# Four neighbouring rows per partition: loads in longer pieces, stores to every fourth row, and a last transpose on TensorE

## The chip, the cores and the metric

The kernel runs on one core of a Trainium2 chip. The metric is the device time of one execution in microseconds (us); the time before is the median of three runs. One further execution was taken by the hardware profiler; its span runs from the first to the last instruction.

## The reference

Attention that keeps the 32 largest scores of each query row, then a feed-forward layer with a squared ReLU. All inputs and the output are float32.

```python
# q, k, v: (8 batches, 8 heads, 576 rows, 64);  w_in: (512, 2048);  w_out: (2048, 512)
scores = scale * np.matmul(q, k.transpose(0, 1, 3, 2))
kth = np.partition(scores, -32, axis=-1)[..., -32:-31]
scores = np.where(scores >= kth, scores, -1e9)
attn = softmax(scores)
x = (attn @ v).transpose(0, 2, 1, 3).reshape(8 * 576, 512)
h = np.maximum(x @ w_in, 0.0)
return (h * h) @ w_out          # (4608, 512)
```

The order of the keys of one head doesn't change a row's result, as long as k and v have the same order. The order of the query rows changes only the row of the output that a result belongs to.

## The kernel before

**A plan, written out.** The kernel first builds a list of operations (`Plan.op`, L73 on), each with an engine, an estimated duration, a priority, the tiles that it reads and writes and the buffers that it takes. `Plan.schedule` (L141) is a list scheduler: it walks through time by events, gives each free engine the ready operation with the lowest priority number, and so fixes the order of the instructions on each of the five queues (PE, ACT, DVE, GpSimd named POOL, and SP for the DMAs). `Emitter` numbers the semaphores and writes the instructions in that order. At run time each engine works through its own list and waits only on semaphores. The scheduler's durations are constants in the code; a load counts the same whatever its pieces are.

**Loads.** A head pair is two heads of one batch. `load_pair` (L653) loads q, k and v of a pair. Four blocks of 128 rows and a rest of 64 rows make up the 576 rows. In the tile of q or k a partition holds five blocks times two heads times 64 elements (`rq`, `rk`: `[P, 5, 2, D]`); in that of v it holds four blocks of the first head, four of the second, and the rests (`rv`: `[P, 10, D]`). A 512-row load gives partition p the rows p, 128 + p, 256 + p and 384 + p:

```python
nc.sync.dma_start(r[:, 0:4, h, :], src[b, 2 * hp + h, r0:r0 + 512, :].rearrange("(tb p) d -> p tb d", p=P))
```

The first pair has its own loads, spread over two queues (`load_first`, L597), with the first block of q by itself (`both`). Its transposes come after ten warm-up matmuls on ones (L1384) in TensorE's order. TensorE transposes each 128-row block (L585), ACT copies the result to `qk`.

**Groups.** A group is 128 query rows of both heads of a pair, or the 64 rest rows of two pairs; there are 144. `score` (L719) makes 576 scores per row and head, ACT copies them to `s` (L755). `top_k` (L835) finds the 32nd largest: DVE folds four quarters of 144 columns into their maxima (L905), POOL gets the smaller ones by integer adds and subtracts (L900), and DVE draws eight maxima at a time (L939, L934, L946) and replaces them (L943). ACT makes the mask `w` from the threshold (L965; L952 and L955 for the last group), TensorE transposes the scores (L585) and adds the mask (L582), ACT takes the exponential `p` (L1021), and `fetch` multiplies by v. Four groups (`HUNT`) get their threshold by a search on ACT and POOL in place of the folds.

**The test and the second plan.** The folds may miss a value, for instance when more than eight of the 32 largest lie in one part. `verdict` (L1388) tests all rows at the end and leaves one flag. If it is set, all engines branch into a second plan (`again`, L1465), which finds all 144 groups' thresholds by full-width maxima and writes all of the output again.

**From attention to the feed-forward layer.** `gather` (L1078) collects the products in `av`. `collect` (L1090) divides by the sums on POOL (L1096) and transposes `x` into `xt` by a DMA (L1109). `feed` (L1121) and, for the last chunk, `feed_last` (L1184) run the two matrix products over chunks of up to 256 rows; `feed_last` accumulates over the head pairs as they come, so that its early matmuls (L1190) need the first two pairs only. In the last chunk the third pair is transposed by TensorE already (L1100), and the fourth in `collect_last` (L1062). Stores go out per 128 rows from two `o` buffers (L1180), for the last chunk in two halves of 256 columns (L1245).

Of the kernel before, what the change touches and what calls it, by code (L numbers as in the profile page):

```python
# [13 lines left out]
P = 128  # L14
# [370 lines left out]
def bass_top_k_attn__then__act_relu_squared_kernel(  # L385
# [8 lines left out]
    NB, H, S, D = q.shape  # L394
# [6 lines left out]
    NHP = 4  # L401
# [187 lines left out]
    def build(full, weights, pl):  # L589
# [7 lines left out]
        def load_first(b, hp, rq, rq2, rk, base):  # L597

            def part(t, src, h, tb, n_):
                r0 = 128 * tb + (64 if h and src is k else 0)  # L600
                return at(t)[:, tb:tb + n_, h, :], src[b, 2 * hp + h, r0:r0 + 128 * n_, :].rearrange(
                    "(tb p) d -> p tb d", p=P)

            def rest(t, src, r0, d0):
                x = src[b, 2 * hp, r0:r0 + 64, :]
                return at(t)[0:64, 4, :, :], bass.AP(x.tensor, x.offset, [x.ap[0], [(S + d0) * D, 2], x.ap[1]])

            def start(queue, *parts):
                return lambda: [queue.dma_start(*x()) for x in parts]

            both = bass.AP(q.tensor, q[b, 2 * hp, 0:P, :].offset, [[D, P], [S * D, 2], [1, D]])
            pl.op("sp", .1, base - 82, start(nc.scalar, lambda: part(rk, k, 0, 0, 4),
                                             lambda: rest(rk, k, REST[0], REST[1] - REST[0])),
                  w=[rk], take=[rk], sem=slot_sem, ndma=2, via="act")
            pl.op("sp", 4.0, base - 81, start(nc.sync, lambda: part(rk, k, 1, 0, 4)), w=[rk], sem=lambda o: "first", ndma=1)
            pl.op("sp", 3.5, base - 80, start(nc.sync, lambda: (at(rq)[:, 0, :, :], both)), w=[rq], take=[rq],
                  sem=slot_sem, ndma=1)
            pl.op("sp", 3.5, base - 79, start(
                nc.sync, lambda: part(rq2, q, 0, 1, 3), lambda: part(rq2, q, 1, 1, 3), lambda: rest(rq2, q, 512, 0)),
                w=[rq2], take=[rq2], sem=slot_sem, ndma=3)  # L620
# [32 lines left out]
        def load_pair(b, hp, base):  # L653
# [3 lines left out]
            def load(t, src, rest):  # L657
                def fn():
                    r = at(t)
                    res = []  # L660
                    for h in range(2):
                        r0 = 64 if h and rest != (512, 512) else 0
                        res.append(nc.sync.dma_start(r[:, 0:4, h, :], src[b, 2 * hp + h, r0:r0 + 512, :].rearrange(
                            "(tb p) d -> p tb d", p=P)))
                    x = src[b, 2 * hp, rest[0]:rest[0] + 64, :]
                    res.append(nc.sync.dma_start(r[0:64, 4, :, :], bass.AP(
                        x.tensor, x.offset, [x.ap[0], [(S + rest[1] - rest[0]) * D, 2], x.ap[1]])))
                    return res
                return fn

            def loadv():
                r = at(rv)
                res = [nc.sync.dma_start(r[:, 4 * h:4 * h + 4, :], v[b, 2 * hp + h, 64 * h:64 * h + 512, :].rearrange(
                    "(tb p) d -> p tb d", p=P)) for h in range(2)]

                for h in range(2):
                    res.append(nc.sync.dma_start(r[64 * h:64 * h + 64, 8 + h, :], v[b, 2 * hp + h, REST[h]:REST[h] + 64, :]))
                return res
# [411 lines left out]
        def collect(got, tt, quick):  # L1090

            avs, nu, xr = got["avs"], got["n"], tile("x")
            r0, rzs_ = units(nu)
            rz = pl.op("dve", .07 + .0045 * nu, tt + 4, lambda: vec.reciprocal(rzall[:, r0:r0 + nu], at(avs)[:, 0:nu, 64]), r=[avs], late=LATE if not quick else 0)
            rzs.append(rz)
            pl.op("gp", .14 + .108 * nu, tt + 4, lambda: gp.tensor_tensor(  # L1096
                at(xr)[:, 0:nu, :], at(avs)[:, 0:nu, 0:64], rzs_, ALU.mult), r=[avs], w=[xr], take=[xr], after=[rz])
            (gi, u0, n_, (xt, col, first), hp) = got["parts"][0]
            if quick == 2 and hp == NHP - 2:
                x = Tile(psum)  # L1100
                pl.op("pe", .1, tt - 30, lambda: tr(half(x)[:, 0:64 * nu], flat(xr, 0, nu), ident_bf[:, :]), r=[xr], w=[x], take=[x])
                return [pl.op("act", .35, tt - 30, lambda: act.copy(
                    at(xt)[:, hp, col:col + 64 * nu], half(x)[:, 0:64 * nu]), r=[x], w=[xt])]
            ops = []
            rows = [p for p in got["parts"] if p[0] != Z]
            if rows:
                _, u0, n_, (xt, col, first), hp = rows[0]
                assert [p[1:3] + (p[4],) for p in rows] == [(u0, n_, hp), (u0 + n_, n_, hp + 1)]
                ops += 2 * [pl.op("sp", 2.0, tt + 5, lambda u0=u0, n_=n_, xt=xt, col=col, hp=hp: [nc.sync.dma_start_transpose(  # L1109
                    at(xt)[:, hp:hp + 2, col:col + 64 * n_].rearrange("p a (i q) -> p (a i) q", q=P) if n_ == 4 else  # L1110
                    at(xt)[:, hp:hp + 2, col:col + 64 * n_], flat(xr, u0, 2 * n_))], r=[xr], w=[xt],
                    take=[xt] if first else [], ndma=1, bw=.25 * n_, sem=lambda o: f"x{xr.slot}")]
# [6 lines left out]
            return ops  # L1119

        def feed(chunk, xt, tm, step):  # L1121

# [34 lines left out]
            for tb in range((nt + 127) // 128):  # L1157
# [17 lines left out]
                for b_, r0, m_ in chunk:  # L1175
                    lo_, hi_ = max(at_, 128 * tb), min(at_ + m_, 128 * tb + n_)
                    if lo_ < hi_:
                        rows.append((lo_ - 128 * tb, hi_ - lo_, S * b_ + r0 + lo_ - at_))
                    at_ += m_
                pl.op("sp", 2.3, to + lag + 4 * step + 1, lambda ob=ob, rows=rows: [nc.sync.dma_start(  # L1180
                    out[row:row + m_, :], at(ob)[p0:p0 + m_, :]) for p0, m_, row in rows],
                    r=[ob], ndma=len(rows), sem=lambda o: f"o{o.tiles[0].slot}")

        def feed_last(chunk, xt, tt, turns):  # L1184
# [56 lines left out]
            for e in range(2):  # L1241
# [1 line left out]
                pl.op("act", .42, tt, lambda e=e, half_=half_: act.copy(  # L1243
                    at(ob)[0:nt, half_], bank(ops[e])[0:nt, 0:256]), r=[ops[e]], w=[ob])
                pl.op("sp", 2.3, tt + e, lambda half_=half_: [nc.sync.dma_start(  # L1245
                    out[S * b + q0:S * b + q0 + nt, half_], at(ob)[0:nt, half_])], r=[ob], ndma=1, sem=lambda o, e=e: f"oe{e}")

        xts = [None] * len(CHUNKS)
        turned = {}
# [276 lines left out]
```

## Time and profile before

| | |
|---|---|
| median of three runs | 775.21 us (775.09 to 775.52) |
| profiled execution | 774.41 us |
| its span | 772.6 us |
| busy: DVE, ACT, PE, POOL | 751.6, 717.9, 713.3, 687.6 us |
| DMA moved | 52.63 MB, 145,033 packets, of which 137,088 under 512 B |

Read it so: four engines are busy for nine tenths of the span or so, and DVE for 97% of it. An edit that shortens a transfer matters where an engine that sets the end waits for it; so the places to look at are the waits for DMAs, and the two ends of the span, where DVE isn't busy yet or any more.

### The profile page before, as it was taken

How to read it: one execution, taken by the hardware profiler on the slowest of the kernel's cores; microseconds unless marked ns; L12 is line 12 of the kernel's file. 1: busy time of each engine (PE TensorE's matmuls, PEld its weight loads, DVE VectorE, ACT ScalarE, POOL GpSimd, SP SyncE). 2: the span in 40 equal slices, each digit the busy share in tenths (PEclk: the TensorE clock that was granted, in tenths of full speed). 3: DMA queues.
4: the chain of work that ended last, by engine and by line, in shares of the span. 5: the costliest groups of instructions: out<-in, count | busy, mean ns of one | idle time of the engine just before them, and what ended most of it. 6: DMA issues, size and time to landing. Idle time of an engine off the chain costs nothing.

```text
span 772.6 us, 27813 instructions
## 1 busy us (share of the span) xinstructions
PE 713.3 (92%) x10680; PEld 528.2 (68%) x10680; DVE 751.6 (97%) x3589; ACT 717.9 (93%) x1141; POOL 687.6 (89%) x720
## 2 busy tenths in 40 slices
PE   7888888999989999998999889999899999999999
PEld 3656666666666676666767657686677777767776
DVE  5999999999999999999999999899999999999996
ACT  4799989899899999999999999999999999998884
POOL 4898998889789899989999899899999998989991
PEclk9999999999999999999999999999999999999999
DMA  7657452032400134103340043301332021100101
GB/s 191 182 137 196 132 135 52 23 83 48 114 11 9 51 83 95 32 16 85 70 99 10 18 111 86 69 6 46 93 82 67 11 68 38 34 23 23 36 23 34
DMA packets 145033, 52.63 MB, mean 68 GB/s; under 512 B 137088, under 2 KB 137344, under 8 KB 144896
## 3 DMA queue, kind: packets, MB, share of 16 engines
q1 hardware_dynamic: 144224, 50.66, 26.7%
q8 instruction: 84, 1.38, 0.8%
q14 instruction: 53, 0.43, 0.2%
q10 hardware_dynamic: 672, 0.16, 0.1%
HBM read 36.70 MB, written 9.44 MB: 60 GB/s over the span
## 4 chain that ended last, share of the span: by engine, by line
ACT 58%; PE 31%; DVE 8%; issue 2%; DVEq 0%; ACTq 0%
PE ps L582 26%; ACT w L965 13%; ACT p L1021 12%; ACT s L755 12%; ACT g L1140 7%; PE ps L585 5%; ACT hz L776 4%; ACT g L1155 3%; DVE f L943 2%; DVE f L905 2%; ACT o L1172 2%; DVE c L939 2%; ACT av L1087 2%; ACT qk L711 1%; ACT qk L712 1%
## 5 line engine op out<-in xcount | busy, mean ns | idle before, releaser
L900 POOL TENSOR_TENSOR f<-u,f 128x864 int32<-128x864 int32 x138 | 236.7, 1715 | 7.6
L965 ACT ACTIVATE w<-s,kth 128x576 bf16<-128x576 f32 x278 | 220.2, 829 | 3.5 <-DVE kth L946 3.5
L943 DVE MATCH_REPLACE8 f<-c,f 128x98 f32<-128x98 f32 (+2 forms) x840 | 221.2, 270 | 0.0
L939 DVE MAX8 c<-f 128x8 f32<-128x98 f32 (+2 forms) x840 | 201.5, 272 | 0.0
L582 PE MATMUL ps<-qk 64*128 64x384 f32 (+3 forms) x1280 | 179.5, 427 | 6.9 <-DVE f L905 5.8
L900 POOL TENSOR_TENSOR u<-f,s 128x576 int32<-128x576 int32 x138 | 166.5, 1206 | 16.6 <-DVE f L905 15.9
L1021 ACT ACTIVATE p<-ps 128x1152 bf16<-128x1152 f32 x144 | 169.1, 1174 | 12.5 <-PE ps L582 11.9
L755 ACT COPY s<-ps 128x1152 f32<-128x1152 f32 x140 | 162.0, 1157 | 17.3 <-PE ps L582 16.9
L582 PEld LDWEIGHTS ps<-qk 64*128 64x128 f32 (+1 forms) x1280 | 130.5, 175 | 39.6 <-DVE f L905 11.8
L582 PE MATMUL ps<-wo,g 128*128 128x512 bf16 (+1 forms) x592 | 142.9, 375 | 2.7 <-ACT qk L714 1.2
L582 PE MATMUL ps<-xt,win 128*128 128x256 bf16 (+1 forms) x1280 | 132.5, 252 | 8.5 <-ACT g L1140 3.6
L900 POOL TENSOR_TENSOR u<-s 128x288 int32<-128x288 int32 x138 | 110.2, 799 | 29.8 <-ACT s L755 26.5
L905 DVE TENSOR_TENSOR f<-ps,f 128x288 f32<-128x288 f32 x280 | 123.7, 442 | 0.1
L946 DVE MAX8 kth<-f 128x8 f32<-128x296 f32 x280 | 120.7, 456 | 0.0
L585 PEld LDWEIGHTS ps<-ident,s 64*128 64x128 f32 x2520 | 96.8, 139 | 30.9 <-ACT w L965 15.1
L582 PEld LDWEIGHTS ps<-xt,win 128*128 128x128 bf16 x1280 | 97.2, 98 | 29.3 <-ACT g L1140 6.0
L934 DVE MAX8 f<-f 128x8 f32<-128x288 f32 x280 | 114.7, 447 | 0.0
L585 PE MATMUL ps<-ident,s 64*128 64x64 f32 x2520 | 107.0, 227 | 4.6 <-ACT w L965 4.1
L1152 POOL TENSOR_TENSOR g<-g 128x512 bf16<-128x512 bf16 x86 | 89.4, 1042 | 2.9 <-ACT g L1140 2.6
L582 PEld LDWEIGHTS ps<-wo,g 128*128 128x128 bf16 x592 | 49.6, 98 | 55.2 <-issue 5.7
L1140 ACT ACTIVATE g<-ps 128x512 bf16<-128x512 f32 x140 | 86.2, 641 | 1.0 <-PE ps L582 0.9
L582 PEld LDWEIGHTS ps<-vb,p 128*128 128x128 bf16 (+1 forms) x1600 | 54.0, 100 | 32.7 <-ACT g L1140 10.5
(104 smaller groups left out, 859.1 us busy)
## 6 DMA issues: line engine op xcount, KB each, us to landing
rv<-in_v_dram SPq DMA_DIRECT2D x64, 128.0 KB, 2.4
rk<-in_k_dram SPq DMA_DIRECT2D x63, 128.0 KB, 2.5
rq<-in_q_dram SPq DMA_DIRECT2D x62, 128.0 KB, 2.5
out_dram<-o SPq DMA_DIRECT2D x31, 256.0 KB, 2.2
g<-in_moe_w_in_dram SPq DMA_DIRECT2D x8, 512.0 KB, 4.2
g<-in_moe_w_out_dram SPq DMA_DIRECT2D x8, 512.0 KB, 4.3
out_dram<-o SPq DMA_DIRECT2D x10, 128.0 KB, 2.3
rq<-in_q_dram SPq DMA_DIRECT2D x32, 32.0 KB, 2.5
```

The lines of the kernel that those rows point to most:

```text
L582: return pe.matmul(o, l, r, start=start, stop=stop, skip_group_check=True)
L585: return pe.matmul(o, i, ident, is_transpose=True, skip_group_check=True, **kw)
L755: cp = [pl.op("act", 1.1, tg - LEAD + 1, lambda: act.copy(at(st)[:, :, 0:S], two(banks(ss)[:, FIRST_AT:], SECOND, S)), r=[ss], w=[st])]
L900: return pl.op("gp", dur, prio, lambda: gp.tensor_tensor(o().bitcast(I32), x().bitcast(I32), y().bitcast(I32), op), **kw)
L905: return dve(.36, lambda: vec.tensor_tensor(o(), two(banks(ss)[:, FIRST_AT + c:], SECOND, QUART), x(), ALU.max), r=[ss], **kw)
L934: prev[i] = [dve(.065 + HALF / 960, lambda i=i: vec.max(at(f)[:, i, A + 7:A - 1:-1], at(f)[:, i, M + QUART:E]), after=prev[i] + [low], hol ...
L939: lambda i=i, t=t, c0=c0, c1=c1: vec.max(eighth(t, i), at(f)[:, i, c0:c1]),
L943: lambda i=i, t=t, c0=c0, c1=c1: vec.match_replace(at(f)[:, i, c0:c1], eighth(t, i), at(f)[:, i, c0:c1], NEG), hold=[f])]
L946: ks.append(chain(kth, i, prev[i], .065 + (8 + HALF) / 960, lambda i=i: vec.max(eighth(kth, i), at(f)[:, i, A:M + QUART]), hold=[f]))
L965: masks[i:] = [pl.op("act", .77, tw + .8 * i, lambda i=i: act.activation(at(wt)[:, i, :], at(st)[:, i, 0:S], ACTF.Relu, bias=kth[:, i, n:n ...
L1021: return act.activation(at(pt)[:, :, :].rearrange("p c (h q) -> p h c q", h=2), bass.AP(x.tensor, x.offset, [x.ap[0], [APART, 2], [64, 9], ...
L1140: return act.activation(at(g)[:, 0:kf * nt], bank(hh)[:, 0:kf * nt], ACTF.Relu)
```

## The change

Three edits come together.

First, the 512-row loads of q, k and v give partition p the four neighbouring rows 4p to 4p + 3, which are 1 KB in a row in DRAM, in place of four rows that lie 128 apart. Block tb of a tile then holds the rows 4p + tb. For the first pair, block 0 of q is still loaded by itself, in 256 B rows that lie 1 KB apart, and the other three blocks in pieces of 768 B.

Second, the output rows of such a block go to every fourth row of the batch's 512 (`block`). The 64 rest rows stay where they are.

Third, `collect` transposes the first two head pairs of the last chunk by TensorE into PSUM, one operation with two transposes, and ACT copies both to `xt` in one instruction. There is no DMA for them any more. The third pair goes through the same code with one transpose. Both operations have a priority ahead of all others that are ready then.

No constant of the planner is changed. The core of the diff:

```diff
         def load_first(b, hp, rq, rq2, rk, base):
             def part(t, src, h, tb, n_):
-                r0 = 128 * tb + (64 if h and src is k else 0)
-                return at(t)[:, tb:tb + n_, h, :], src[b, 2 * hp + h, r0:r0 + 128 * n_, :].rearrange(
-                    "(tb p) d -> p tb d", p=P)
+                r0 = 64 if h and src is k else 0
+                return at(t)[:, tb:tb + n_, h, :], src[b, 2 * hp + h, r0:r0 + 512, :].rearrange(
+                    "(p tb) d -> p tb d", p=P)[:, tb:tb + n_, :]
...
-            both = bass.AP(q.tensor, q[b, 2 * hp, 0:P, :].offset, [[D, P], [S * D, 2], [1, D]])
+            both = bass.AP(q.tensor, q[b, 2 * hp, 0:P, :].offset, [[4 * D, P], [S * D, 2], [1, D]])
...
                         res.append(nc.sync.dma_start(r[:, 0:4, h, :], src[b, 2 * hp + h, r0:r0 + 512, :].rearrange(
-                            "(tb p) d -> p tb d", p=P)))
+                            "(p tb) d -> p tb d", p=P)))
...
                 res = [nc.sync.dma_start(r[:, 4 * h:4 * h + 4, :], v[b, 2 * hp + h, 64 * h:64 * h + 512, :].rearrange(
-                    "(tb p) d -> p tb d", p=P)) for h in range(2)]
+                    "(p tb) d -> p tb d", p=P)) for h in range(2)]
...
-            if quick == 2 and hp == NHP - 2:
-                x = Tile(psum)
-                pl.op("pe", .1, tt - 30, lambda: tr(half(x)[:, 0:64 * nu], flat(xr, 0, nu), ident_bf[:, :]), r=[xr], w=[x], take=[x])
-                return [pl.op("act", .35, tt - 30, lambda: act.copy(
-                    at(xt)[:, hp, col:col + 64 * nu], half(x)[:, 0:64 * nu]), r=[x], w=[xt])]
+            if quick == 2:
+                x, m = Tile(psum), nu // 2
+                def turns():
+                    for i in range(m):
+                        ins = tr(half(x)[:, P * i:P * i + P], flat(xr, 2 * i, 2), ident_bf[:, :])
+                    return ins
+                pl.op("pe", .1 * m, tt - 30, turns, r=[xr], w=[x], take=[x])
+                return m * [pl.op("act", .14 + .105 * m, tt - 30, lambda: act.copy(
+                    at(xt)[:, hp:hp + m, col:col + P], half(x)[:, 0:P * m].rearrange("p (a q) -> p a q", q=P)),
+                    r=[x], w=[xt], take=[xt] if first else [])]
...
+        def block(b, r0, m):
+            if r0 >= 512:
+                return out[S * b + r0:S * b + r0 + m, :]
+            return out[S * b:S * b + 512, :].rearrange("(p tb) d -> tb p d", tb=4)[r0 // P]
...
-                    out[row:row + m_, :], at(ob)[p0:p0 + m_, :]) for p0, m_, row in rows],
+                    block(b_, row, m_), at(ob)[p0:p0 + m_, :]) for p0, m_, b_, row in rows],
...
-                    out[S * b + q0:S * b + q0 + nt, half_], at(ob)[0:nt, half_])], r=[ob], ndma=1, sem=lambda o, e=e: f"oe{e}")
+                    block(b, q0, nt)[:, half_], at(ob)[0:nt, half_])], r=[ob], ndma=1, sem=lambda o, e=e: f"oe{e}")
```

More of the change, by code (lines that the diff above doesn't have):

```diff
@@ L1119, in collect @@
             return ops
+        def block(b, r0, m):
+            if r0 >= 512:
+                return out[S * b + r0:S * b + r0 + m, :]
+            assert m == P and r0 % P == 0
+            return out[S * b:S * b + 512, :].rearrange("(p tb) d -> tb p d", tb=4)[r0 // P]
         def feed(chunk, xt, tm, step):
@@ L1177, in feed @@
                     if lo_ < hi_:
-                        rows.append((lo_ - 128 * tb, hi_ - lo_, S * b_ + r0 + lo_ - at_))
+                        rows.append((lo_ - 128 * tb, hi_ - lo_, b_, r0 + lo_ - at_))
                     at_ += m_
                 pl.op("sp", 2.3, to + lag + 4 * step + 1, lambda ob=ob, rows=rows: [nc.sync.dma_start(
-                    out[row:row + m_, :], at(ob)[p0:p0 + m_, :]) for p0, m_, row in rows],
+                    block(b_, row, m_), at(ob)[p0:p0 + m_, :]) for p0, m_, b_, row in rows],
                     r=[ob], ndma=len(rows), sem=lambda o: f"o{o.tiles[0].slot}")
```

## Prediction

> **What bounds the kernel now.** I read the page first: the span, and what the DMA engines do.
>
> ```profile
> span 772.6 us, 27813 instructions
> ...
> DMA  7657452032400134103340043301332021100101
> ...
> q1 hardware_dynamic: 144224, 50.66, 26.7%
> ```
>
> The 16 DMA engines are on average a quarter busy; only the first slices are full. Then the busy time of the vector engine in three stretches (length of the stretch, busy time, instructions, granted TensorE clock, DMA share, GB/s):
>
> ```profile
> 0.00:8.90 8.90, 0.86 (x3) 1.00 0.59 132
> 8.90:758.50 749.60, 743.35 (x3560) 1.00 0.28 68
> 758.50:772.60 14.10, 7.40 (x28) 1.00 0.13 44
> ```
>
> From 8.90 to 758.50 us DVE is busy for 743.35 of 749.60 us. Its order is written out beforehand, so there it is the clock of the kernel, and a change can take at most the 6.25 us of idle time out of that stretch. The waits say who ended the idle time, for DVE (first two rows) and for every engine that waited for a DMA (last three):
>
> ```profile
> DVE f L905 <- ACT s L755: 3.5, 5, 2.6
> DVE f L943 <- POOL f L900: 2.8, 2, 1.9
> ...
> POOL vb L715 <- DMA rv<-in_v_dram: 4.9, 1, 4.9
> POOL vb L647 <- DMA rv<-in_v_dram: 1.0, 1, 1.0
> PE ps L582 <- DMA rq<-in_q_dram: 0.2, 1, 0.2
> ```
>
> No row has DVE wait for a DMA. The three waits for loads came once each, none in the steady state; in the one of 4.9 us POOL has nothing else to do yet, since the first two groups get their minima from DVE (L915, L918). Two ends are left where DVE is not the bound: the start and the tail.
>
> **The start.** The chain of waits begins with TensorE's warm-up matmuls; the timeline shows when the first loads are issued and the first pair is transposed:
>
> ```profile
> 1.06 3.81 PE ps L582 x10
> 4.88 0.93 PE ps L585 x6
> ...
> 8.90 0.47 DVE f L905
> ```
>
> ```profile
> 1.27 2.34 SPq L609 DMA_DIRECT2D rq<-in_q_dram  x4
> ...
> 4.72 0.33 PE L585 MATMUL ps<-ident,rq 128*128 128x128 f32 x1
> ```
>
> ```profile
> rv<-in_v_dram SPq DMA_DIRECT2D x64, 128.0 KB, 2.4
> ...
> rv<-in_v_dram SPq DMA_DIRECT2D x64, 16.0 KB, 2.2
> ...
> rq<-in_q_dram SPq DMA_DIRECT2D x1, 64.0 KB, 2.8
> ...
> rk<-in_k_dram ACTq DMA_DIRECT2D x1, 32.0 KB, 3.3
> ```
>
> The ten warm-up matmuls end as the transposes begin: 1.06 + 3.81 = 4.87, then 4.88. The first q block, issued at 1.27, landed 2.8 us later, at 4.07, 0.65 us before its transpose at 4.72. The matmuls stand ahead of the transposes in PE's order and depend on no load. So a load that lands sooner starts nothing sooner, and DVE's first fold stays at 8.90.
>
> **The change, part by part.**
>
> *Loads.* 32 head pairs times 3 tensors times 1,024 pieces are 98,304 of the 144,224 packets; cut to a quarter they fall by 73,728. In a quiet queue a 128 KB load lands in 2.4 us against 2.2 for 16 KB, so the shorter transfer is worth some 0.2 us per load. The planner has the same operations with the same costs, so every engine keeps its order, and no engine waits for these loads after the start. I cost it at **0**; bounds: −1.1 (all of 3.3 − 2.2 gained at the start, were the loads the holder after all) and +0.3 (a first load nearly a microsecond later than now, which uses up the 0.65 us). SP issues as many loads as before, in the same places.
>
> *Stores.* Pieces stay 2 KB (1 KB for the last two), with a row pitch of 8 KB in place of 2 KB. Two o buffers cover all stores but the last ones:
>
> ```profile
> out_dram<-o SPq DMA_DIRECT2D x10, 128.0 KB, 2.3
> ...
> 768.38 0.81 SPq L1245 DMA_DIRECT2D out_dram<-o  x2
> ```
>
> They end the span (768.38 + 0.81 + 2.3 = 771.5 of 772.6). No row shows a wider pitch; I take **0**, with bounds of ±0.2 (the spread of 2.4 and 2.2 above), far end +2.3 in a rival.
>
> *The transposes of the tail.* Removed is SP's transpose of the first two head pairs of the last chunk; added are two 128x128 bf16 transposes on PE and a 128x256 copy on ACT, ahead of everything by priority. The timeline there:
>
> ```profile
> 756.46 0.61 POOL L1096 TENSOR_TENSOR x<-av,rzall 128x256 bf16<-128x256 f32 x1 [0.47 <-DVE rzall L1094]
> ...
> 757.01 1.47 PE L582 MATMUL ps<-wo,g 128*128 128x512 bf16 x6
> ...
> 757.10 1.17 SPq L1109 DMA_TRANSPOSE xt<-x  x1
> 757.12 1.13 ACT L1021 ACTIVATE p<-ps 128x1152 bf16<-128x1152 f32 x1 [1.37 <-PE ps L582]
> ...
> 757.64 0.83 DVE L946 MAX8 kth<-f 128x8 f32<-128x296 f32 x2
> 758.15 0.77 ACT L952 ACTIVATE w<-s,kth 128x576 bf16<-128x576 f32 x1
> ...
> 758.82 0.34 ACT L955 ACTIVATE w<-s,kth 128x64 bf16<-128x64 f32 x1
> 759.06 0.57 ACT L1172 COPY o<-ps 128x512 f32<-128x512 f32 x1
> ...
> 759.12 0.49 PE L582 MATMUL ps<-vb,p 128*128 128x65 bf16 x10
> 759.54 0.29 PE L582 MATMUL ps<-steep_bf,w 64*128 64x64 bf16 x8
> ...
> 759.64 0.27 ACT L1087 COPY av<-ps 128x130 f32<-128x130 f32 x1
> ...
> 759.94 1.07 PE L582 MATMUL ps<-xt,win 128*128 128x128 bf16 x16
> ...
> 760.04 1.13 ACT L1021 ACTIVATE p<-ps 128x1152 bf16<-128x1152 f32 x1
> ```
>
> The matmuls that used the DMA's result (L582 xt,win at 759.94) follow the mask matmuls without a gap: PE had no wait there to remove. The path of the tail is DVE's last threshold (ends 758.47), w, the mask, the last exponential p at 760.04. Now x is ready at 757.07; its transposes fall among the three pairs of wo matmuls that run from 757.01 on; their copy is ready while ACT computes p and is next at 758.15, ahead of w. Prices:
>
> ```profile
> L585 PE MATMUL ps<-ident_bf,x x2: 219/220/220, 760.8 to 762.6; 128*128 128x128 bf16 x2
> ```
>
> ```profile
> L1243 ACT COPY o<-ps 128x256 f32<-128x256 f32 x2 | 0.7, 372 | 2.0 <-PE ps L582 2.0
> ...
> L1102 ACT COPY xt<-ps 128x128 bf16<-128x128 bf16 x1 | 0.3, 265 | 0.0
> ```
>
> Two transposes take 0.2 to 0.4 us of PE (219 ns each, pipelined or not). The copy is between 0.27 and 0.37 us; I take 0.37, which in ACT's back-to-back flow (w's 0.77 us hold the next off for 758.82 − 758.15 = 0.67) is 0.27. So w and its second part come 0.27 later and end at 759.43 in place of 759.16. The mask began 0.38 us after that end, right behind the vb matmuls on PE (759.12 + 0.49), so part of the 0.27 is covered; what isn't delays the mask and then p. If the cover takes all, or if the early matmuls, ready sooner, get out of the way of the last ones, the cost is 0. If o and av, which are queued between w and p on ACT, push p as a block, all 0.37 comes through, and with PE's transposes 0.6 at most. I take about half of 0.27, **+0.15**, with bounds 0 and +0.6. SP loses 1.17 us of issue in a stretch where its next item is a store that waits for o.
>
> *Sum.* Profiled execution 774.41 us, 1.81 us outside its span; 0 + 0 + 0.15 gives 774.56. The median of the runs, 775.21, lies 0.80 above it, so I forecast **775.4 us**.
>
> **The rivals.**
>
> *A, the start was held by the loads.* Against: 4.87 and 4.88. For: the 3.3 us of the 32 KB k load, issued behind another. Price at most −1.1: 774.3. [...] Chance 0.07.
>
> *B, the fallback.* The fast pass folds 576 columns into four quarters (L900 to L946) and afterwards tests every row (L1389 to L1418); one row that fails sends all engines through the second, full plan. New rows per partition mean other keys in each fold. Over 3 million random placements of the 32 largest among 576 columns, taken through these folds, 12 break a test; times 36,864 query rows that is 0.15 rows expected, and the four searched groups add about 0.03 the same way. Chance of at least one: 0.15. Price, from the one row with a maximum over the whole width:
>
> ```profile
> L814 DVE MAX8 hk<-hz 128x8 f32<-128x576 f32 x8 | 5.7, 746 | 0.4 <-POOL hz L812 0.4
> ```
>
> Per group the second plan has 8 maxima over 576 columns and 6 replacements over as many; with all 14 at 0.746 us, 144 groups take 1,500 us, 860 us with the maxima alone: about 2,280 us. It decides from one row on; this is the case on the slow side.
>
> *C, the loads aren't cut to a quarter.* A q or k tile holds the two heads' rows alternately, 256 B each, so the writing side may keep the pieces small and only v's merge (24,576 fewer packets). The time stays 775.4. Chance 0.06.
>
> *D, fewer DMA packets close DVE's idle time.* At most 6.25 us: 769.2. Against it: the releasers are ACT and POOL. Chance 0.03.
>
> *E, stores of wide pitch land late.* Were the last landing doubled, +2.3: 777.7; it leaves the band when 2.3 becomes 3.9. [...] Chance 0.02.
>
> **How the numbers follow.** Forecast 0.67, A 0.07, B 0.15, C 0.06, D 0.03, E 0.02. Within 0.2% (1.55 us, about what a measurement of this kernel can tell from no change) lie the forecast, A and C: 0.80. Faster: D, 0.03. Slower: B and E, 0.17. The range goes from 775.2 − 1.1 − 0.1 = 774.0 to 775.2 + 0.6 + 0.3 + 0.2 + 0.2 = 776.5, the last 0.2 for the scatter of runs; it leaves out B, D and E, 0.20.
>
> **What would show it.** The first DVE fold stays at 8.90 and DVE's busy time between its ends at 743. Packets fall by some 73,700 (by 24,600 under C). One DMA transpose fewer, four ident_bf transposes on PE, and the last p near 760.2. A first fold before 8.5 would show A right and my reading of the warm-up wrong; MAX8 over 576 columns after 770 us would show B; a p before 760.0 would mean that the copy found a hole that I don't see.

## The result and the profile after

The changed kernel takes **777.47 us** (median of 20 runs, 775.45 to 779.60) against 775.08 us for the kernel before in the same series (20 runs, 774.34 to 776.56): a ratio of 1.0029, 95% interval 1.0022 to 1.0037 (the ratio is estimated from all runs and is not the quotient of the two medians). It is 2.4 us slower. The forecast was 775.4 us, in a range from 774.0 to 776.5. The profiled execution of the changed kernel took 779.0 us, with a span of 777.1.

The page of the changed kernel, on the span, TensorE's instructions and the DMA traffic (packets, then MB and GB/s; for a queue: packets, MB, share of the 16 DMA engines):

```profile
span 777.1 us, 27815 instructions
...
PE 715.5 (92%) x10681; PEld 529.7 (68%) x10681; DVE 752.5 (97%) x3589; ACT 718.5 (92%) x1142; POOL 687.7 (88%) x720
...
DMA packets 120169, 52.57 MB, mean 68 GB/s; under 512 B 104032, under 2 KB 112480, under 8 KB 120032
...
q1 hardware_dynamic: 119360, 50.59, 25.3%
q8 instruction: 84, 1.38, 0.7%
```

Packets of q1 fell from 144,224 to 119,360, by 24,864. That is v's 24,576 and the small change of the tail; q's and k's packets did not merge. The busy time of DVE between the same marks as before:

```profile
0.00:8.90 8.90, 0.86 (x2) 1.00 0.48 117
8.90:758.50 749.60, 739.57 (x3536) 1.00 0.26 68
```

In 749.60 us DVE now idles 10.03 us instead of 6.25; 0.88 us of it lie before its first fold, which comes at 9.78 instead of 8.90. The waits say for whom:

```profile
DVE f L905 <- ACT s L755: 6.3, 11, 2.6
...
PE ps L582 <- issue: 1.5, 1, 1.5
```

DVE waited for the scores 6.3 us instead of 3.5. The other row is new: TensorE stood still once, for 1.5 us, and the releaser is called "issue", which only says that no semaphore event was found to end the wait. For TensorE no row names a DMA as long as that. The timeline names the place. Before, SP's queue and TensorE near 120 us:

```profile
116.70 0.94 SPq L663 DMA_DIRECT2D rk<-in_k_dram  x2
117.68 0.63 SPq L666 DMA_DIRECT2D rk<-in_k_dram  x1
118.35 1.28 SPq L1109 DMA_TRANSPOSE xt<-x  x1
...
121.36 0.46 DVE L905 TENSOR_TENSOR f<-ps,s 128x288 f32<-128x288 f32 x1
121.39 0.61 PE L582 MATMUL ps<-xt,win 128*128 128x256 bf16 x4
...
126.57 0.45 DVE L905 TENSOR_TENSOR f<-ps,s 128x288 f32<-128x288 f32 x1
```

The same instructions after:

```profile
119.02 1.25 SPq L663 DMA_DIRECT2D rk<-in_k_dram  x2
120.30 0.63 SPq L666 DMA_DIRECT2D rk<-in_k_dram  x1
120.98 1.29 SPq L1116 DMA_TRANSPOSE xt<-x  x1
...
123.68 0.46 DVE L905 TENSOR_TENSOR f<-ps,s 128x288 f32<-128x288 f32 x1
...
125.33 0.60 PE L582 MATMUL ps<-xt,win 128*128 128x256 bf16 x4 [1.46 <-issue]
...
129.36 0.46 DVE L905 TENSOR_TENSOR f<-ps,s 128x288 f32<-128x288 f32 x1 [0.39 <-ACT s L755]
```

Read it in this order. The two 128 KB k loads of one head pair take 1.25 us to issue where they took 0.94. So the transpose of `xt` behind them stands 123.68 − 120.98 = 2.70 us ahead of the DVE fold of that moment, where it stood 121.36 − 118.35 = 3.01 ahead. By the landing times of this tile in this stretch it lands 4.3 us after its issue where it landed after 2.5: 1.8 us for a delay of 0.31. TensorE's matmul on `xt`, due with the fold, waits 1.46 us; the scores behind it come late, and DVE waits. The fold is 2.32 us behind its counterpart at 123.68 and 2.79 behind at 129.36; the next one of its kind (132.06 before, 135.22 after) is 3.16 behind. So this place costs **0.84 us**.

The other differences of the two profiled executions lie elsewhere: 0.89 us at the first fold (8.90 against 9.78), about 0.9 and 1.4 us around 70 and 565 us, where TensorE's granted clock fell to a half for 3.4 us. What of this belongs to the change, only the other kernels can tell.

### The profile page after: what moved, and what is told of

It reads as the page before. It is cut to its first block, busy times and chain, and to the rows that moved or that the text cites. A ratio compares the mean times of both kernels' runs of the same rounds, so it can differ in the third digit from the quotient of the medians.

```text
span 777.1 us, 27815 instructions
## 1 busy us (share of the span) xinstructions
PE 715.5 (92%) x10681; PEld 529.7 (68%) x10681; DVE 752.5 (97%) x3589; ACT 718.5 (92%) x1142; POOL 687.7 (88%) x720
## 3 DMA queue, kind: packets, MB, share of 16 engines
q1 hardware_dynamic: 119360, 50.59, 25.3%
## 4 chain that ended last, share of the span: by engine, by line
ACT 57%; PE 26%; DVE 12%; POOL 3%; issue 2%; DVEq 0%; POOLq 0%; ACTq 0%
PE ps L582 22%; ACT w L965 13%; ACT p L1021 12%; ACT s L755 11%; ACT g L1153 6%; PE ps L585 5%; ACT hz L776 4%; DVE f L943 3%; DVE f L905 3%; ACT g L1168 3%; DVE c L939 2%; ACT av L1087 1%; ACT o L1185 1%; DVE kth L946 1%; ACT qk L711 1%
```

## The experiments

The 16 kernels ran in four series, each beside the kernel before in the same series (775.04, 775.17, 775.06 and 774.83 us, 26 to 35 runs each). Times are medians of 6 to 12 runs; ratios are to the kernel before, with the 95% interval, estimated as above.

### Which edit is it?

**tail_only**: the kernel before with the third edit alone.

```diff
-            if quick == 2 and hp == NHP - 2:
+            if quick == 2:
+                x, m = Tile(psum), nu // 2
```

> Loads theory (the q and k loads got dearer, and they make the start and some transposes late): the tail's edit alone costs little, +0.1 to +0.2 us against before (775.2). Clock theory (TensorE's half-clock episodes of 3.4 us fall at random, and the changed kernel only drew more of them): also within 0.3 us of before. Tail theory (the copy on ACT holds up the last group): +1.5 to +2.3, about 777.4.

Measured: 775.52 us, 0.9999 [0.9989, 1.0009].

**stores_only**: the kernel before with the output rows at every fourth row.

```diff
-                    out[row:row + m_, :], at(ob)[p0:p0 + m_, :]) for p0, m_, row in rows],
+                    block(b_, row, m_), at(ob)[p0:p0 + m_, :]) for p0, m_, b_, row in rows],
```

> Only the stores go to every fourth row, so the output's rows are in another order. Loads and clock theory: as before within 0.3 us (775.1), landing 2.2 to 2.3 us. Store theory (rows of a wide pitch land late, also in the way of loads): +0.5 to +2, landing 2.6 or more.

Measured: 774.75 us, 0.9992 [0.9982, 1.0003].

**v_only**: the kernel before with the new v loads.

```diff
                 res = [nc.sync.dma_start(r[:, 4 * h:4 * h + 4, :], v[...].rearrange(
-                    "(tb p) d -> p tb d", p=P)) for h in range(2)]
+                    "(p tb) d -> p tb d", p=P)) for h in range(2)]
```

> Only v's loads take four neighbouring rows, so v's rows don't match the keys. All theories: as before within 0.3 us (775.1); landing 2.2 us in place of 2.4, some 24,600 packets fewer. The loads theory would allow a gain of 0.1 to 0.3 where v's transfers no longer hold others up.

Measured: 775.22 us, 0.9994 [0.9984, 1.0004], with 120,457 packets: nearly the whole fall of packets is v's, and it is worth nothing.

**qk_only**: the kernel before with the new q and k loads, those of the first pair too.

```diff
                         res.append(nc.sync.dma_start(r[:, 0:4, h, :], src[...].rearrange(
-                            "(tb p) d -> p tb d", p=P)))
+                            "(p tb) d -> p tb d", p=P)))
```

> Only the loads of q and k (first pair and all others) take four neighbouring rows per partition; v and the stores are as before, so v's rows and the output rows don't match. Loads theory: most of the loss is here, +1.5 to +2.3 us (776.6 to 777.4), first fold of DVE after 9.3 us in place of 8.90, landing 2.8 us in place of 2.5, and waits of TensorE for transposes behind such loads. Clock theory: within 0.5 us of before, unless the episodes are more here too. Tail theory: as before, 775.1.

Measured: 776.73 us, 1.0019 [1.0008, 1.0031], with 145,033 packets, exactly as many as before. So the loss is that of the q and k loads, and they got no larger packets. Its `xt` near 121 us lands in 4.5 us, and TensorE waits 1.74 us. Its first fold comes at 9.17 us, a little earlier than forecast.

**qk_undone**: the changed kernel with the old q and k loads.

> The changed kernel with q's and k's loads put back to rows that lie 128 apart (v, the stores and the tail stay changed, so the rows don't match and the output is another). Loads theory: back at before, 774.8 to 775.5, xt transposes at about 120 us landing in 2.5 us, no wait of TensorE over 1 us there. Clock theory (what is left is only the number of half-clock episodes): as the changed kernel, 777.

Measured: 775.01 us, 0.9992 [0.9982, 1.0001]. Taking the q and k edit out takes the loss out.

**rest_qk_only**: as qk_only, but the first pair keeps its old loads (the one line of qk_only's diff, without `load_first`).

> Before with the new q and k loads for all head pairs but the first (v, the stores and the first pair as before, so the output is another). Loads theory, one late place near 125 us: +1.1 to +1.7 (776.2 to 776.8), the wait of some 1.5 us for xt there again, and a first fold whose time goes with the length of the ten warm-up matmuls alone. If the first pair's loads were the cause: as before, 775.0.

Measured: 778.90 us, 1.0040 [1.0029, 1.0052]. The loss doesn't need the first pair. It is 2.1 us above the upper end of the forecast: eight of the twelve runs have two or more half-clock stretches of TensorE, while the two runs at full clock took 776.87 and 777.09 us (what these stretches cost is the subject of the last part of this section).

### What is it about these loads?

A new q or k load reads 1 KB in a row and writes it as four pieces of 256 B, since the tile holds the two heads' rows alternately. **side_by_side** is the changed kernel with the 1 KB written in a row too, for all pairs but the first; q and k then lie in other places than the transposes read them from.

```diff
-                        res.append(nc.sync.dma_start(r[:, 0:4, h, :], src[...
+                        res.append(nc.sync.dma_start(r[:, :, :, :].rearrange("p a h d -> p (a h) d")[:, 4 * h:4 * h + 4, :], src[...
```

> The changed kernel, but q's and k's loads (first pair excepted) write the four rows of a head side by side in the tile, 1 KB on both sides. The transposes read the tile as before, so rows of two heads are mixed and the output is another. If uneven pieces are the cause: issue back to some 0.45 us per load, landing 2.2 us, some 48,000 packets fewer than the changed kernel, and a time of 774.8 to 775.5. If any load of four neighbouring rows is dearer: 776.5 to 777.5 as the changed kernel.

Measured: 775.57 us, 0.9997 [0.9988, 1.0006]. Its packets and the same stretch of the timeline:

```profile
DMA packets 72553, 52.57 MB, mean 68 GB/s; under 512 B 40544, under 2 KB 64864, under 8 KB 72416
```

```profile
117.86 0.81 SPq L663 DMA_DIRECT2D rk<-in_k_dram  x2
118.71 0.63 SPq L666 DMA_DIRECT2D rk<-in_k_dram  x1
119.40 1.26 SPq L1116 DMA_TRANSPOSE xt<-x  x1
...
122.55 0.61 PE L582 MATMUL ps<-xt,win 128*128 128x256 bf16 x4
```

With 1 KB on both sides the packets do fall by 72,480, as the prediction had it, the pair of loads issues in 0.81 us instead of 0.94, `xt` lands in 2.5 us, and the loss is gone. There is no gain beside it: half the packets of the kernel buy nothing.

**split_loads** is the kernel before with each 512-row load of q and k issued as two of 256 rows. The pieces are the old ones, only SP is busier; the plan's durations were kept.

```diff
-                        res.append(nc.sync.dma_start(r[:, 0:4, h, :], src[b, 2 * hp + h, r0:r0 + 512, :].rearrange(
-                            "(tb p) d -> p tb d", p=P)))
+                        for c in (0, 2):
+                            res.append(nc.sync.dma_start(r[:, c:c + 2, h, :], src[b, 2 * hp + h, r0 + 128 * c:r0 + 128 * c + 256, :].rearrange(
+                                "(tb p) d -> p tb d", p=P)))
```

> Before, each 512-row load of q and k (first pair excepted) issued as two loads of 256 rows, with the old rows and the old pieces of 256 B; the plan's order and costs are unchanged. It adds issue time on SP without any piece that is read and written in different lengths. If the time that SP needs per load is what makes the transposes late: as bad as the new loads or worse, +1 to +3 (776 to 778), with the wait near 125 us. If it is the uneven pieces as such on the DMA engines: as before, 775.0 to 775.5.

Measured: 778.77 us, 1.0039 [1.0024, 1.0054]; the k loads of that pair take 1.91 us to issue, `xt` lands 4.1 us after its issue, and TensorE waits 2.02 us; the time is above the 778 of the forecast. So old pieces with a longer issue lose as well: a longer time on SP ahead of the transpose was enough here. That it is the same lateness as in after isn't shown by this; the packets below show a difference.

### Is it one place or all of them?

**one_pair_undone** is the changed kernel with the k and v loads of a single head pair of 32 in the old form, the pair whose k loads stand ahead of `xt` near 120 us. **one_pair_only** is the reverse: the kernel before with only these loads new. k and v of the pair change together.

```diff
-            rq, rk, rv = tile("rq"), tile("rk"), tile("rv")
+            rq, rk, rv = tile("rq"), tile("rk"), tile("rv"); one = state["pairs"] == 10
...
-                            "(p tb) d -> p tb d", p=P)))
+                            "(tb p) d -> p tb d" if one and src is k else "(p tb) d -> p tb d", p=P)))
...
-                    "(p tb) d -> p tb d", p=P)) for h in range(2)]
+                    "(tb p) d -> p tb d" if one else "(p tb) d -> p tb d", p=P)) for h in range(2)]
```

> The changed kernel, with the k and v loads of one head pair of 32 (the eleventh, whose k loads stand on SP right ahead of the transposes near 120 us) in their old form, rows 128 apart; its q loads stay new. If the loss comes about at this one place: the two k loads take 0.94 to 1.15 us to issue there instead of 1.25, the xt transpose behind them lands in 2.5 us instead of 4.3, TensorE goes on without a wait near 125 us, and the time is that of the kernel before, 775.2 (within 0.6). If the loss is spread over the q and k loads of all pairs, one of 32 gives back a thirtieth of it: 777.4.

> The kernel before, with the k and v loads of that one head pair alone in the new form; all other loads, the stores and the tail are the old ones. One place: the xt transpose lands in 4 us or more, TensorE waits 1.4 to 2 us near 123 us, and the time is 776.5 to 778.9, as with all q and k loads new. Loss spread over all pairs: 775.2 to 775.3.

Measured: one_pair_undone 775.20 us, 1.0000 [0.9989, 1.0010]; one_pair_only 776.80 us, 1.0021 [1.0011, 1.0032]. The timeline of one_pair_undone:

```profile
117.34 0.92 SPq L663 DMA_DIRECT2D rk<-in_k_dram  x2
...
118.98 1.28 SPq L1116 DMA_TRANSPOSE xt<-x  x1
...
122.03 0.61 PE L582 MATMUL ps<-xt,win 128*128 128x256 bf16 x4
```

and that of one_pair_only:

```profile
118.77 1.26 SPq L663 DMA_DIRECT2D rk<-in_k_dram  x2
...
120.75 1.28 SPq L1109 DMA_TRANSPOSE xt<-x  x1
...
125.21 0.60 PE L582 MATMUL ps<-xt,win 128*128 128x256 bf16 x4 [1.60 <-issue]
```

Two k loads out of 63 (and the pair's v loads, of a kind that v_only shows to cost nothing) bring the loss and take it away. The other 30 pairs' slower loads (over all k loads that L663 issues, the median issue of one is 0.63 us in after, 0.51 in before) cost nothing that can be measured. **after_again** is the changed kernel once more, beside these:

> The changed kernel once more, beside the three others: 777.5 (777 to 778), the xt transpose near 121 us lands in 4 us or more, and TensorE waits there for 1.4 to 1.8 us; half-clock stretches of 3.4 us at other places than in its first profile.

Measured: 777.87 us, 1.0033 [1.0020, 1.0046]; `xt` lands in 4.1 us, TensorE waits 1.31 us, a little less than forecast.

### Why does the transpose land 1.8 us late for a delay of 0.3?

Right behind `xt` SP issues the transposes of the rest rows (`xz`). **xz_waits** is the changed kernel in which these wait until `xt` has landed.

```diff
-                        ..., ndma=2, bw=1.0, sem=lambda o, hp=hp: f"z{xr.slot}_{hp}"))
+                        ..., ndma=2, bw=1.0, after=ops[:1], sem=lambda o, hp=hp: f"z{xr.slot}_{hp}"))
```

> The changed kernel, in which each transpose of the rest rows (xz) is issued only when the transpose of the other rows of the same head pairs (xt) has landed; on SP other loads move in between. If xt lands late because xz is issued right behind it: near 121 us xt lands in 2.5 us, TensorE doesn't wait, and the time falls to 775.2 to 775.6. If xt is late by itself, behind the slower loads: it still lands in over 4 us, and the time stays near 777.5 or above.

Measured: 777.66 us, 1.0027 [1.0017, 1.0038].

```profile
120.72 1.28 SPq L1116 DMA_TRANSPOSE xt<-x  x1
122.05 2.17 SPq L663 DMA_DIRECT2D rq<-in_q_dram  x2
124.26 0.63 SPq L666 DMA_DIRECT2D rq<-in_q_dram  x1
...
125.06 0.60 PE L582 MATMUL ps<-xt,win 128*128 128x256 bf16 x4 [1.46 <-DMA xt<-x]
```

With plain loads behind it `xt` still lands after 4.2 us, so the theory that `xz` holds it up falls. As a gain, the wait now has its name: it is `xt`'s DMA.

The trace's records of single packets showed what the kernels with a late `xt` have in common. Besides the data there are packets of 4 B, 32 for `xt` (in before 1.9 to 2.2 us after its issue), and the semaphore that tells of its landing goes up in 16 steps behind them (2.35 to 2.51 us). So these packets are taken for reports, two for each sixteenth of the transfer. On queue 8 there are blocks of 16,384 B called "instruction". They are taken for TensorE's code, by their number: the page has 84 of them, and 10,681 matmuls and as many weight loads are 21,362 instructions, 254 per block. One such block is on its way while `xt` is. In after it is under way from 123.08 to 124.15 us, and for this stretch the row of that queue is

```profile
q8 instruction: 1, 0.02, 6.3%
```

6.3% of 16 engines is one engine, busy with that one packet. Times in us from `xt`'s issue; "reports late" are those of the 32 that come after 2.3 us:

| kernel | `xt` lands | code block | reports late, at |
|---|---|---|---|
| before | 2.5 | 2.37 to 3.77 | none |
| one_pair_undone | 2.5 | 2.38 to 3.68 | none |
| v_only | 2.5 | 2.92 to 3.85 | none |
| side_by_side | 2.5 | 2.37 to 3.64 | none |
| after | 4.3 | 2.10 to 3.17 | 2, at 3.16 and 3.17 |
| after_again | 4.1 | 2.00 to 3.02 | 2, at 3.00 to 3.02 |
| xz_waits | 4.2 | 2.14 to 3.07 | 2, at 3.06 and 3.07 |
| one_pair_only | 4.4 | 2.08 to 3.29 | 2, at 3.28 and 3.29 |
| qk_only | 4.5 | 2.50 to 3.42 | 2, at 3.41 and 3.42 |
| rest_qk_only | 4.6 | 1.99 to 3.39 | 2, at 3.58 and 3.59 |
| split_loads | 4.1 | 1.31 to 2.68 | 11, at 3.49 to 3.51 |

In the six kernels from after to rest_qk_only, 30 of the 32 reports of `xt` are in by 2.2 us, as all 32 are in before, and the last two come at the end of the code block or up to 0.2 us behind it. Two of 32 are a sixteenth, and the block kept 6.3% of 16 engines busy, so I read it as one engine of 16 that moved the block first; the records don't say which engine moved a packet. In after, the semaphore of the transfer agrees: 15 of its 16 steps come by 2.64 us, the last at 4.25. The transfer counts as landed about 1.1 us after the block's end. split_loads is another case: 11 reports come late, 0.8 us after the block's end, and all 16 steps of the semaphore come at 4.0 us or later. (rest_qk_only has the two late reports, but all its 16 steps come after 4.4 us.) In the kernels that lose nothing, two late reports come as well, but 0.1 us after the block's end and among those of `xz`, for which nobody waits. TensorE's wait is for `xt`, not for the block: xz_waits has it as 1.46 us with the DMA of `xt` as releaser.

If that is the cause, moving the block must move the landing with no load touched. The planner's fillers (three matmuls on the identity whose result nobody reads, put in where TensorE would have little to do) allow it: five groups of them between 23 and 40 us get five matmuls (before_more and after_more, shown here) or one (before_less and after_less). With their weight loads that is 20 instructions more or fewer, about 0.8 us of TensorE's code (an estimate from the ten blocks of after between 21.8 and 123.1 us, one every 10.1 us for 256 instructions), with the order of everything else as it was.

```diff
     def spare(tl):
-        for _ in range(3):
+        spared.append(tl)
+        for _ in range(5 if len(spared) <= 5 else 3):
```

> The kernel before, with five matmuls instead of three in the same five filler groups: 20 TensorE instructions more ahead of 120 us, so TensorE's code blocks are fetched some 0.8 us earlier against the work. All loads are the old ones. Theory, race with the code block: the fetch starts some 1.6 us after xt's issue instead of 2.4, xt lands in over 4 us, TensorE waits there for 1.4 to 2 us, and the time is 776.5 to 779. Rival, the k loads make xt late: it lands in 2.5 us, 775.2.

> [...] Theory, a race of the xt transpose with the code block: the fetch now starts some 2.9 us after xt's issue instead of 2.1, xt lands in 2.5 us, TensorE doesn't wait near 125 us, and the time is 775.0 to 776.0. Rival, xt is late behind the slower k loads by itself: xt lands in over 4 us, 777.5.

> Control: the changed kernel with the 20 TensorE instructions more of before_more. Race with the code block: the fetch starts some 1.3 us after xt's issue, as in split_loads, xt lands in over 4 us, and the time stays at 777.5 (777 to 779). Were the fillers by themselves what moves the time, it would move here as in before_more, to 779.

> Control: the kernel before with the 20 TensorE instructions fewer of after_less. Race with the code block: the fetch starts some 3.2 us after xt's issue, xt lands in 2.5 us as now, and the time stays at 775.2 (774.8 to 775.6).

Measured:

| kernel | time, ratio | `xt` lands | code block | reports late, at | TensorE waits |
|---|---|---|---|---|---|
| before_more | 776.18, 1.0020 [1.0007, 1.0033] | 4.1 | 1.22 to 2.62 | 11, at 3.42 to 3.45 | 0.97 |
| after_less | 781.32, 1.0070 [1.0049, 1.0090] | 5.0 | 2.96 to 3.89 | 2, at 3.88 | 2.20 |
| after_more | 776.53, 1.0013 [1.0001, 1.0025] | 4.2 | 1.48 to 2.68 | 9, at 3.48 to 3.51 | 1.36 |
| before_less | 777.69, 1.0037 [1.0023, 1.0050] | 2.5 | 2.36 to 3.80 | none | 0 |

The timeline of before_more:

```profile
117.13 0.93 SPq L663 DMA_DIRECT2D rk<-in_k_dram  x2
...
118.77 1.28 SPq L1109 DMA_TRANSPOSE xt<-x  x1
...
122.95 0.60 PE L582 MATMUL ps<-xt,win 128*128 128x256 bf16 x4 [0.97 <-PE ps L582]
```

and that of after_less:

```profile
121.95 1.28 SPq L1116 DMA_TRANSPOSE xt<-x  x1
...
127.03 0.60 PE L582 MATMUL ps<-xt,win 128*128 128x256 bf16 x4 [2.20 <-issue]
...
131.07 0.46 DVE L905 TENSOR_TENSOR f<-ps,s 128x288 f32<-128x288 f32 x1 [1.13 <-ACT s L755]
```

before_more is the clear case: with the old loads and their old issue time (0.93 us) the block comes earlier, `xt` lands in 4.1 us instead of 2.5, and TensorE waits. Its lateness is that of split_loads, with 11 late reports and all steps of the semaphore after 3.9 us. It costs DVE less than in after, since `xt` still stands 3.0 us ahead. The controls came out as forecast in the landing, 4.2 and 2.5 us (though the block of before_less came at 2.36, not at 3.2). The times of before_more and after_more lie 0.3 and 0.5 us below their forecasts. after_less didn't come out as forecast: the block came 0.86 us later, but `xt` still came behind it and landed 0.7 us later too, 1.1 us after the block's end as in after. So in these kernels a late landing follows the block; but whether `xt` is late is not settled by the start of the block's packet alone (v_only's block starts at 2.92 and `xt` lands in 2.5; after_less' starts at 2.96 and qk_only's at 2.50, and `xt` lands in 5.0 and 4.5). What settles it stays open.

By these kernels alone a rival would stand: after_less and qk_only fit one in which the new k loads by themselves make one engine late. The other `xt` transposes in the same traces decide against it. Here are all 693 of the 18 traces, by when a code block begins after their issue (the bounds were chosen from the same data):

| code block begins, us after `xt`'s issue | `xt` | landed after more than 3.2 us | median landing |
|---|---|---|---|
| -0.5 to 1.0 | 124 | 58 | 3.15 |
| 1.0 to 2.2 | 78 | 78 | 3.94 |
| 2.2 to 2.35 | 8 | 3 | 2.44 |
| 2.35 to 3.1 | 106 | 4 | 2.43 |
| none of these | 377 | 19 | 2.45 |

Of the 19 in the last row 18 are one and the same transpose near 95 us, once in each kernel. Of the 78, 31 stand in kernels with the old q and k loads, and all 78 landed 1.0 to 1.5 us after the block's end but for one. Before has nine late ones among 39, after nine among 38. The row of before's `xt`:

```profile
DMA to landing us min/median/max: 2.3/2.5/4.1
```

So neither new loads nor a long issue are needed for a late `xt`, and in these two traces the change didn't make them more frequent. It brought one such meeting to a transpose that has only half a microsecond to spare.

The totals of the two kernels with fewer fillers can't be read against the forecast, for a reason found only in their tails: from the last store's issue to the end of the span pass 777.9 − 770.76 = 7.1 us in before_less and 780.8 − 773.74 = 7.1 in after_less, against 772.6 − 768.38 = 4.2 before and 777.1 − 773.13 = 4.0 after. With 20 instructions fewer, the program's end took 2.9 us longer. In these two, TensorE's last code block before the end is fetched only 4.4 and 4.0 us after the last store's issue (775.16 to 776.08 and 777.78 to 779.00 us); before and after have theirs on its way when that store is issued (767.56 to 768.72 and 772.50 to 773.71). That suggests that the end waits for code; no run tests it. Without the 2.9 us they would be at 774.8 and 778.4.

### What the wait costs in all

The place itself took 0.84 us in after's profile, and the median is 2.4 up. The rest goes with TensorE's clock. Here is the profile of after near 565 us (length, PE busy and instructions, PEld, DVE, ACT, POOL, granted clock, DMA share, GB/s):

```profile
560.00:564.00 4.00, 3.12 (x40) 2.35 (x42) 4.00 (x21) 4.00 (x10) 3.77 (x4) 0.81 0.61 134
564.00:568.00 4.00, 4.00 (x64) 3.11 (x57) 3.04 (x14) 2.86 (x5) 2.71 (x4) 0.76 0.50 123
```

and that of before near 22 us:

```profile
20.00:24.00 4.00, 3.58 (x35) 2.93 (x30) 3.90 (x19) 2.51 (x4) 2.95 (x3) 0.64 0.99 259
```

In each of these stretches the clock was halved for 3.41 us on end. In before's profile this came once, early, and cost nothing; in after's it came at 67.6 and 562.5 us, and DVE lost about 0.9 and 1.4 us beside it. Among after's 20 runs the seven with a mean clock of 1.0 have a median of 776.12 us, 1.04 above the kernel before; the 13 with one to three such stretches (0.998 to 0.993) have 778.52. So about 1.0 us is the wait, and the rest of the 2.4 is half-clock stretches. Kernels with the old loads show them too (tail_only at 67.1 and 562.0 us, v_only at 27.2 and 68.2), so the change doesn't cause them alone. In rest_qk_only one begins at 124.9 us and in split_loads at 126.9, right at TensorE's wait, which suggests that the wait drew it. But the one of after at 67.6 us begins ahead of the wait, so the wait can't have drawn that.

For the 20 runs of before beside the result the clocks are not in the records; for its 122 runs in the other four series they are. Of these, 60 ran at full clock, with a median of 775.0 us, so that the seven of after at full clock lie 1.1 us above. Nine of the 122 have a mean clock of 0.996 or less, which is two stretches or more. Of the kernels whose `xt` lands in time near 120 us it is 4 of 70 runs; of those where TensorE waits for it, after among them, 41 of 106 (the two kernels with fewer fillers are left out). So more of these stretches go with the late `xt`. Why isn't settled.

## Why the prediction was wrong

**The failed step** is the one on the loads: "The planner has the same operations with the same costs, so every engine keeps its order, and no engine waits for these loads after the start. I cost it at 0". The order was kept and indeed no engine waits for a load. But near 120 us the pair of 128 KB k loads takes 0.31 us longer to issue on SP (1.25 against 0.94), behind them in SP's queue stands a transpose that TensorE waits for, and with the 0.31 us it met a block of TensorE's code (2.10 to 3.17 us after its issue) and landed 1.8 us late. The step looked for who waits for the loads; it had to look for who waits for what is queued behind them. The sentence "SP issues as many loads as before, in the same places" counts instructions where it had to count their time, and no row of before had the time of a load with unequal pieces: that was an unknown cost and had no bound.

**Landing times.** "The shorter transfer is worth some 0.2 us per load" held for v alone. The issue rows of after:

```profile
rv<-in_v_dram SPq DMA_DIRECT2D x64, 128.0 KB, 2.2
...
rk<-in_k_dram SPq DMA_DIRECT2D x63, 128.0 KB, 2.8
```

v fell from 2.4 to 2.2 us, k rose from 2.5 to 2.8.

**Rival C** (the writing side keeps q's and k's pieces small, only v's merge) was right in its mechanism and its count, at a chance of 0.06, but it gave "the time stays 775.4". The text had the reason for C in the tile's layout in hand; it should have been the forecast. Its time was wrong by the same step as above.

**The start** was read rightly for the kernel before: loads don't hold it. In after the first fold came at 9.78 us instead of 8.90, but the chain shows longer warm-up matmuls ahead of it:

```profile
1.06 4.45 PE ps L582 x10
5.51 1.18 PE ps L585 x6
...
9.78 0.47 DVE f L905
```

The same ten matmuls took 3.81 us before. The first record of a granted clock of 1.0 stands at 4.1 us there and at 6.1 us here (called "clock up" below). In before seven of the ten matmuls, from 1.1 to 4.0 us, take 627 ns on average and the last three 390; here all ten take 632 on average, and the first three transposes behind them 421 to 474, the fifth 273. The fold follows that moment in kernels of both loads: 9.54 us in tail_only, which has the old ones (clock up at 5.6), 9.99 in v_only (6.7). The 8.90 of the profile before was an early case; rival A's price wasn't there. But in after_again, where the clock came up early, the new loads did hold the start. It came up at 3.8 us and the warm-up matmuls ended at 4.77; the first q block, issued at 1.52 instead of 1.27, landed 3.6 us later instead of 2.8, and TensorE waited for it:

```profile
5.17 0.30 PE L585 MATMUL ps<-ident,rq 128*128 128x128 f32 x1 [0.41 <-PE ps L582]
```

The first fold came at 9.21. The bound of +0.3 for "a first load nearly a microsecond later than now" was this case.

**The stores** cost nothing, as forecast (stores_only). Rival E is out.

**The tail** cost what was forecast. In after's timeline DVE's last maxima, the copy, w and the last p:

```profile
762.28 0.83 DVE L946 MAX8 kth<-f 128x8 f32<-128x296 f32 x2
762.78 0.37 ACT L1108 COPY xt<-ps 128x256 bf16<-128x256 bf16 x1
763.04 0.79 ACT L952 ACTIVATE w<-s,kth 128x576 bf16<-128x576 f32 x1
...
764.80 1.13 ACT L1021 ACTIVATE p<-ps 128x1152 bf16<-128x1152 f32 x1
```

From DVE's last threshold to p pass 764.80 − 763.11 = 1.69 us, against 760.04 − 758.47 = 1.57 before: +0.12, where +0.15 was taken. The copy takes the 0.37 us forecast, ahead of w.

**Rivals B and D.** No group went through the second plan. D said that fewer packets would close DVE's idle time; with 72,480 fewer (side_by_side) the time stayed.

**The range** ended at 776.5, with the unknown loads at +0.3 at most. The true term was about +1.1 at full clock, of which 0.84 are seen at the place, and +1.3 in runs with half-clock stretches. The room of the transpose would not have shown it by itself: before, SP leaves `xt` 121.36 − 118.35 = 3.01 us for a landing of 2.5, and the half microsecond to spare is more than the 0.31 lost. The longest landing would have: before's trace has `xt` landing in up to 4.1 us, so a bound of 4.1 − 3.01 = 1.1 us stood in the profile.

## What to carry to other kernels

A load that nobody waits for still takes time on the queue that issues it (here 1.25 us for two, where it was 0.94), so ask for each changed transfer what stands behind it there and how much room that has, against the longest landing of its kind and not the median. In these loads pieces merged only where both ends were contiguous: a longer run on one side alone left the packets as they were (145,033 in before and in qk_only) and made the issue longer (1.25 us against 0.94). And fewer packets were worth nothing here, where before had three waits for loads in all (4.9, 1.0 and 0.2 us, none of them DVE's): 72,480 of 145,033 fewer left the time at 0.9997 [0.9988, 1.0006] (side_by_side).

## What the runs showed of the hardware that was not expected

- Near 120 us, two 128 KB loads in 256 B pieces on both sides issue in 0.94 us; read in 1 KB and written in 256 B, in 1.25; in 1 KB on both sides, in 0.81. Over the whole kernel the median landing is 2.5, 2.8 and 2.3 us.
- A DMA transpose (`xt`) landed after 3.4 to 4.6 us instead of some 2.4 in all 78 cases in which a 16 KB code block began 1.0 to 2.2 us after its issue. A block is under way for 0.9 to 1.7 us in after. With 84 blocks in 777 us, one every 9.3 us, an `xt` with little room can meet one, and adding 20 instructions some 80 us earlier changed which one did (before_more).
- TensorE's clock was halved for 3.41 us at a time in kernels that keep it busy for 92% of the span. The moment at which the clock comes up at the start scatters from run to run, from 3.8 us (after_again) to 7.0 (after_less).
- 20 TensorE instructions fewer made the program's end 2.9 us longer, from the last store's issue to the last instruction, in both kernels that had them.
